# A new order of the same operations on all engines, with 26 warming matmuls, in a fused attention and mixer kernel

## The chip, the cores and the metric

The kernel runs on one core of a Trainium2 chip. The metric is device time in microseconds (us), the median of three runs. Beside the runs there is one profiled execution with a trace of every engine and DMA queue.

## What is computed

Eight batches, eight heads, a sequence of 576 and a head dimension of 64. Attention is causal by blocks of 64: a query sees the keys of its own block and of the earlier ones. A mixer follows, first along the sequence (256 hidden), then along the channels (1536 hidden), with a residual each:

```python
scores = scale * np.matmul(q, k.transpose(0, 1, 3, 2))
mask = block_i >= block_j
attn = np.exp(scores - max) / (sum + 1e-09)          # masked scores are -1e9
x = np.matmul(attn, v)                               # as (batch, 576, 512)
h = np.maximum(x.transpose(0, 2, 1) @ w_tok1, 0.0) @ w_tok2
u = x + h.transpose(0, 2, 1)
h2 = np.maximum(u @ w_ch1, 0.0) @ w_ch2
return u + h2
```

Inputs and the output are float32.

## The kernel before

The whole kernel is a list of some 1500 operations (`Plan`, `P.add`). One operation is a small piece of work on one engine: a set of score matmuls, an exponential, a load, an evacuation of a PSUM bank. Each states its dependencies, the engines that it may run on, and the banks that it takes and gives back.

Which engine runs an operation, which bank it gets and where it stands are written out in one long string, `ORDER` (L97 to L178), and `Plan.placed()` walks along it. A word of it is the operation's number, a letter for the engine (T TensorE or PE, A ScalarE or ACT, D VectorE or DVE, P GpSimd or POOL, S SyncE or SP), and one letter for each PSUM bank taken: a to d are the "mm" banks, e to h the "late" ones, s and t the two score tiles of two banks each. Each engine works through its words strictly in this order, and an instruction that waits holds up all that stands behind it on the same engine. That goes for DMA issues too: the loads of q, k, v and weights are issued by POOL or SP between that engine's other work. Nothing is decided while the kernel runs.

The stages of one batch, with their lines:

- Load: `load_qk` casts and loads q and k, L395 for the cast, L419, L426 and L437 for the DMA issues, L442 for the transposes on DVE. `load_v` is L471, the channel weights are L505 and L514.
- Attention: `score_set` (L569) makes eight or so products of 32 rows with q and k, in PSUM; an exponential on ACT (L587 and L737 in the first batch, L776 later) turns them to bf16; the end block is copied and cleared (L595, L600, `tail`); `head_out` (L617) and `ends_out` (L670) multiply by v, with a column of ones for the sum; a reciprocal and a product on DVE (L637, L643) normalize.
- Token mixing: `token_up` (L811, L815) and `token_mix` (L910). For the first batch `first_u` (L846, L859, L871) brings the result into the transposed form through PE; for later batches SP issues DMA transposes (L977, operations 606 and 607 among them).
- Channel mixing: `channel_up` (L1038), `channel_up_half` (L1111) and `channel_up_fast` (L1235) going up, with relu at L797; `first_down` (L1460) and `channel_down_fast` (L1369) going down. The fast forms save matmuls with sums of operands that DVE makes (L1351) and with folds of the products on DVE (L1393). The stores are L1421 and L1435, 128 or 256 KB or 512 KB each.

The last batches have no attention beside them, so the end of the kernel is a long row of products, folds and stores.

At the start nothing has landed yet, and PE has nothing to do. `raise_clock` gives it matmuls on a tile of zeros: `WARM` = 11 of 512 columns in one operation (43, L366), and after that single operations (44 to 80, L373) of 256 columns, "keep" matmuls, which `ORDER` strews among the first score sets. `init_tiles` (L340) clears the tile of zeros and four other tiles on DVE.

Operations that the prediction names: 17 and 14 are the first casts on ACT, 13 and 16 the loads ahead of them; 15, 18, 20, 22, 24 and 1, 2 are transposes on DVE and clears; 138, 142, 161 and 163 score sets of the first batch; 200 and 205 the two score sets behind these that take four banks each; 51 and 58 keep matmuls, 150 and 173 attention outputs, 154 and 165 likewise; 9 the clearing of the zeros; 850, 853 and 847 loads of q and k for later batches; 1460, 1462, 1492 and 1484 products of the last stage, and 1461 (which 1462 waits for), 1485 and 1475 folds there.

Of the kernel before, what the change touches and what calls it, by code (L numbers as in the profile page):

```python
# [27 lines left out]
class Plan:  # L28
# [69 lines left out]
    16S 0A 11D 10D 13S 9D 21P 1D 2D 43Ta 5D 19P 4D 3D 23P 33P 27P 14A 25P 31P 15D 29P 17A 20D 37P 44Tb 45Tb 46Tb 22D  # L98
    47Ta 36P 48Ta 49Ta 18D 50Ta 51Ta 52Ta 35P 53Ta 24D 54Ta 55Ta 56Ta 125Ts 34P 100Ttbc 179P 126A 28D 57Ta 58Ta 59Ta
    176P 60Ta 61Ta 26D 62Ta 101A 12P 106Ts 63Ta 32D 182P 64Ta 107A 65Ta 104Tt 42P 30D 66Ta 67Ta 105A 68Ta 39P 123Ts  # L100
    102D 103D 69Ta 70Ta 41P 119A 71Ta 157Tt 124A 112Td 40P 113T 116Ta 108Tb 114D 120A 38P 109T 115D 138Ts 158A 181D
    81P 72Td 73Tc 74Tc 121D 75Tc 122D 139A 82P 76Tc 7D 144Tt 110D 111D 84P 135Td 178D 127Tc 145A 161Ts 185P 136D
    117D 137D 140D 131Tb 180D 83P 128T 162A 142Tt 177D 90P 132T 129D 143A 77Td 89P 163Ts 130D 133D 86P 134D 78Td
    164A 118D 141D 159D 200Tdcba 160D 85P 203A 173Te 154Tf 165Tg 202A 91P 174D 166T 155D 156D 201A 184D 92P 205Tbhfc
    204A 183D 169Td 88P 170T 209A 167D 263Ta 168D 208A 175D 150Tc 171D 261Tg 172D 207A 187D 267Td 206A 87P 186D
    146Te 262A 147T 264A 151T 268D 237Tgbfh 152D 339P 6D 148D 269Ta 153D 241A 149D 273Td 189P 240A 270D 281Tc 239A
    274D 265Te 190P 238A 271Ta 8D 282D 275Tb 266A 191P 193Tdhfg 276A 272D 283Te 196A 277Tc 342P 194A 315Ta 278D
    306Tb 197A 188P 294Td 195A 279Tc 284A 192P 318Tf 198D 280D 291Tg 319T 348P 316T 309Tc 317A 310T 257D 93P 320A
    307T 295T 94P 308A 292T 311A 258D 225Teahf 345P 296A 300Tb 227A 95P 285Tc 228A 286T 293D 226A 303Td 287D 229A
    304T 351P 232Tahge 341D 199D 312Tc 230D 233A 305D 313T 234A 231D 288Tf 344D 314A 297Ta 340D 236A 289T 343D 235A  # L110
    210Td 513P 245Tc 290A 211D 213Th 516P 212D 242Te 246D 216Tg 354P 247D 301T 214D 215D 248Td 243D 302A 298T 244D
    355P 217D 219Tc 249D 299A 250D 222Th 220D 254Te 221D 363Tdbaf 255D 256D 251Tc 349D 364A 330Te 352P 252D 365A
    218D 253D 321Td 367A 223D 224D 366A 259D 353P 368Tcghb 420Ta 372A 370A 422Tb 347D 371A 525P 346D 322T 421D 423A
    260D 369A 356Tafgh 323T 359A 357A 350D 424Tb 360A 324D 331T 358A 425D 388Tcadg 361P 514D 430Tb 391A 434Th 332T
    389A 431D 435A 518D 426Td 392A 517D 400Thcbf 390A 515D 428Tg 404A 393P 362D 334Ta 522P 403A 429D 677P 401A 335T
    333D 402A 528P 427D 376Tb 373Tc 394D 527P 96D 395Tdfgh 379Te 526P 377D 396A 374D 336T 375D 397A 519P 378D 380D
    405Tc 398A 680P 381D 382Tb 399A 406D 385Td 407D 432Te 337D 417Tc 383D 386D 433A 530Tafgh 387D 384D 418D 436Td
    419D 531A 440Tb 97D 414Tc 534A 325Te 533A 98D 326T 532A 415D 437A 416D 542Tahgf 99D 441A 438Tc 545A 327T 439D
    544A 444D 463Tgd 543A 445D 448Thb 328D 466A 464Tc 451D 546A 329S 411Ta 408Te 465A 446D 469T 412D 690P 413D 449Tf
    523D 470A 454T 529P 450A 409D 442Ta 410D 452Tc 455A 443D 691P 467Tg 520D 453A 537Taefh 447D 692P 468A 456T 521D  # L120
    538A 473T 689P 524D 539A 471T 679D 540A 683P 596Ta 457D 541A 474D 562Tcefh 597A 678D 458T 566A 681D 594Ta 565A
    459D 564A 460D 476T 563A 595D 461T 477A 569Tchfe 682D 462A 472D 604Ta 847P 571A 478Tdb 475D 686P 572A 605D 602Tg
    535P 481A 600Th 603D 536P 570A 598Ta 567P 482Tf 601D 607S 568P 553Tc 844P 599D 483A 479Tg 550Th 554D 555D 480A
    488T 551D 484T 552D 606S 489D 486T 485A 556Tc 487D 491T 573A 574Thadg 557D 490D 492A 547Te 558D 577A 493D 497Tbf
    575A 548D 576A 549D 559Tc 578A 688D 701Tedah 498A 685D 579Tg 560D 704A 684D 499T 705A 494D 850P 702A 693P 580D
    585Ta 703A 581D 503T 500D 687D 706Tgdbh 586D 587D 561D 591Te 504D 710A 501Ta 709A 495D 708A 592D 707A 593D 582Tc
    502D 627Tbd 612The 608D 630A 588Tg 583D 496D 505T 859P 615D 858P 633T 584D 506D 507T 857P 634A 589D 590D 860P
    694Tcgab 508D 856P 618T 698A 849D 509T 697A 846D 696A 619D 695A 760Tb 609D 610D 699P 510D 738Tacgh 761A 848D
# [42 lines left out]
    1457D 1392D 1492The 1453D 1393T 1488D 1493A 1489D 1455D 1498T 1394D 1458T 1396S 1460T 1490D 1459D 1472Tca 1468D  # L171
    1465S 1461D 1494T 1464S 1473A 1469D 1476Td 1470D 1478T 1491D 1462T 1479D 1471D 1499D 1482T 1463D 1496Tg 1477D
    1466S 1483D 1502T 1467S 1497D 1484T 1503D 1500T 1507S 1485D 1495D 1480T 1487S 1501D 1474T 1506S 1481D 1504T
    1475D 1486S 1505D 1508S
"""


@with_exitstack  # L178
def kernel(
# [93 lines left out]
    BANK = ("mm", "late mm", "full", "late")  # L273
# [1310 lines left out]
```

## Time and profile before

| what | value |
|---|---|
| runs | 284.08, 284.12 and 285.28 us, median 284.12 |
| span of the profiled execution | 284.7 us (0.2% above the median; no other time is listed for it) |
| granted TensorE clock, each window | 1.00 |
| busy: PE, weight loads, DVE, ACT, POOL | 275.8, 197.6, 240.3, 180.4, 71.7 us |
| matmuls on PE | 4038, of them 46 on zeros |
| moved by DMA | 31.79 MB |

A row of the profile's timeline gives start and length in us, the engine, the line, the operation with output and inputs, the tile shape, and a count where equal instructions stand together; in brackets is the idle time of the engine just before, with what ended it. "issue" there means that the profile shows nothing that the engine waited for. A row of PE's waits names the line that waited, what for, the total in us, how often, and the longest. A window's row begins with its bounds and length, then busy time and count for PE, weight loads, DVE, ACT and POOL, the granted clock, the share of DMA, and GB/s. The queue q8 carries the instructions themselves from memory.

### The profile page before, as it was taken

How to read it: one execution, taken by the hardware profiler on the slowest of the kernel's cores; microseconds unless marked ns; L12 is line 12 of the kernel's file. 1: busy time of each engine (PE TensorE's matmuls, PEld its weight loads, DVE VectorE, ACT ScalarE, POOL GpSimd, SP SyncE). 2: the span in 40 equal slices, each digit the busy share in tenths (PEclk: the TensorE clock that was granted, in tenths of full speed). 3: DMA queues.
4: the chain of work that ended last, by engine and by line, in shares of the span. 5: the costliest groups of instructions: out<-in, count | busy, mean ns of one | idle time of the engine just before them, and what ended most of it. 6: DMA issues, size and time to landing. Idle time of an engine off the chain costs nothing.

```text
span 284.7 us, 9438 instructions
## 1 busy us (share of the span) xinstructions
PE 275.8 (97%) x4038; PEld 197.6 (69%) x4038; DVE 240.3 (84%) x519; ACT 180.4 (63%) x325; POOL 71.7 (25%) x120
## 2 busy tenths in 40 slices
PE   7998999999999899999999999999999999999994
PEld 3667656556878676987777658744488876468883
DVE  3589569799999799999998997997998987598893
ACT  3798685778888358996879785136546653764000
POOL 8975635170641062060341220000000000000000
PEclk9999999999999999999999999999999999999999
DMA  8999999969989495898199587130033403000246
GB/s 160 166 174 202 190 205 203 137 94 134 144 120 119 71 84 87 225 135 122 11 169 102 87 106 132 49 119 18 2 74 98 126 7 131 12 2 0 104 127 212
DMA packets 64776, 31.79 MB, mean 112 GB/s; under 512 B 53088, under 2 KB 55904, under 8 KB 64736
## 3 DMA queue, kind: packets, MB, share of 16 engines
q0 software_dynamic: 45040, 17.64, 53.1%
q1 hardware_dynamic: 19696, 13.57, 19.6%
q8 instruction: 31, 0.51, 0.7%
q14 instruction: 9, 0.07, 0.1%
HBM read 35.85 MB, written 9.44 MB: 159 GB/s over the span
## 4 chain that ended last, share of the span: by engine, by line
PE 92%; DVE 2%; ACT 2%; DMA 1%; issue 1%; SPq 0%; DVEq 0%
PE late L1369 14%; PE mm L1369 11%; PE late L1235 7%; PE mm L1111 7%; PE late L1111 6%; PE mm L569 6%; PE mm L1235 6%; PE mm L617 4%; PE mm L811 3%; PE mm L910 3%; PE mm L1038 3%; PE late L569 2%; PE late L617 2%; PE late L811 2%; PE mm L1460 2%; PE late L1460 2%
## 5 line engine op out<-in xcount | busy, mean ns | idle before, releaser
L776 ACT ACTIVATE e_sb<-late 128x512 bf16<-128x512 f32 x89 | 50.5, 609 | 10.4 <-PE late L569 9.1
L776 ACT ACTIVATE e_sb<-mm 128x512 bf16<-128x512 f32 x79 | 45.1, 609 | 9.9 <-PE late L569 6.6
L471 POOL DMA_DIRECT2D vals<-in_v_dram x45 | 37.2, 844 | 26.7 <-PE late L617 15.9
L442 DVE STREAM_TRANSPOSE qk_sb<-qk_sb 128x288 int32<-128x288 int32 (+2 forms) x57 | 36.2, 694 | 4.6 <-ACT qk_sb L395 3.5
L1369 PEld LDWEIGHTS <-sums 128*128 128x128 bf16 x288 | 27.6, 98 | 5.6 <-issue 1.8
L1369 PEld LDWEIGHTS <-gT 128*128 128x128 bf16 x288 | 27.8, 98 | 4.6
L569 PEld LDWEIGHTS <-qk_sb 32*64 32x64 bf16 x1280 | 19.9, 104 | 13.1 <-issue 8.8
L569 PE MATMUL mm<-qk_sb 32*64 32x64 bf16 (+7 forms) x546 | 27.8, 291 | 0.0
L569 PE MATMUL late<-qk_sb 32*64 32x512 bf16 (+7 forms) x594 | 27.1, 291 | 0.0
L617 PEld LDWEIGHTS <-e_sb 128*128 128x128 bf16 x640 | 23.8, 97 | 4.1 <-issue 0.9
L1111 PEld LDWEIGHTS <-ws_sb 128*128 128x128 bf16 x192 | 17.8, 98 | 3.4 <-issue 1.3
L797 ACT ACTIVATE gT<-mm 128x512 bf16<-128x512 f32 x25 | 14.7, 601 | 7.8 <-PE mm L1111 3.0
L617 PE MATMUL mm<-vals,e_sb 128*128 128x65 bf16 x430 | 19.0, 193 | 0.0
L643 DVE TENSOR_TENSOR x_sb<-mm,rinv 128x256 bf16<-128x256 f32 x43 | 17.9, 421 | 1.1
L1111 PEld LDWEIGHTS <-wc_sb 128*128 128x128 bf16 x144 | 15.4, 114 | 1.8 <-issue 0.2
L1235 PEld LDWEIGHTS <-ws_sb 128*128 128x128 bf16 x96 | 9.3, 98 | 10.1 <-issue 0.2
L1369 PE MATMUL late<-wd_sb,sums 128*128 128x256 bf16 x108 | 13.6, 272 | 1.2 <-issue 1.2
L1369 PE MATMUL late<-wd_sb,gT 128*128 128x256 bf16 x120 | 14.7, 273 | 0.0
L595 POOL COPY vals<-e_sb 128x256 bf16<-128x256 bf16 x10 | 4.1, 412 | 40.9 <-issue 22.9
L395 ACT COPY mm<-late 128x512 f32<-128x512 f32 x17 | 9.9, 584 | 7.1 <-PE late L1235 5.0
L797 ACT ACTIVATE gT<-late 128x512 bf16<-128x512 f32 x17 | 10.2, 602 | 6.3 <-PE late L1235 3.4
L1235 PE MATMUL late<-e_sb,ws_sb 128*128 128x512 bf16 x44 | 12.6, 379 | 0.0
(203 smaller groups left out, 656.2 us busy)
## 6 DMA issues: line engine op xcount, KB each, us to landing
out_dram<-o_sb SPq DMA_DIRECT2D x14, 512.0 KB, 3.1
vals<-in_v_dram POOLq DMA_DIRECT2D x28, 128.0 KB, 5.4
qk_sb<-in_k_dram POOLq DMA_DIRECT2D x12, 288.0 KB, 6.3
qk_sb<-in_q_dram POOLq DMA_DIRECT2D x12, 288.0 KB, 5.9
out_dram<-o_sb SPq DMA_DIRECT2D x7, 256.0 KB, 3.2
wc_sb<-in_moe_w_ch_dram POOLq DMA_DIRECT2D x8, 192.0 KB, 7.7
wc_sb<-in_moe_w_ch_dram POOLq DMA_DIRECT2D x3, 512.0 KB, 10.4
vals<-in_v_dram POOLq DMA_DIRECT2D x15, 64.0 KB, 4.9
```

The source lines that it names most:

```text
L442: nc.vector.transpose(dst[:, 0:S, :] .rearrange("p s e -> p (s e)") .bitcast(I32) .rearrange("p (a k) -> p k a", k=NB)[:, k0:k1], raw2.bit ...
L471: nc.gpsimd.dma_start(out=t[128 - p : 128, J, hs, 0:64], in_=src)
L569: nc.tensor.matmul(out=home(n)[64 * half : 64 * half + 64, c : c + w], lhsT=bar[r, 0] if j is None else kT[i][r, 64 * j : 64 * j + 64, par ...
L617: nc.tensor.matmul(out=u[:, I, 0:65], lhsT=e[:, h, c : c + 128], rhs=vt[:, J, head, 0:65], start=(J == 0), stop=(J == I),)
L643: nc.vector.tensor_tensor(out=xt[:, 0:4, 64 * head : 64 * head + 64], in0=u[:, :, 0:64], in1=ri[:, 0:4].to_broadcast([128, 4, 64]), op=MULT,)
L776: nc.scalar.activation(dst, bank_of(x), EXP, scale=scale)
L797: nc.scalar.activation(dst, src, RELU)
L811: nc.tensor.matmul(out=ps, lhsT=w1_sb[:, c, tt : tt + 255 : 2], rhs=xt[:, c, cols], start=(c == 0), stop=False)
L1111: nc.tensor.matmul(out=bank_of(bank)[:, 256 * o_ : 256 * o_ + 256], lhsT=x(o_, m), rhs=y[:, :, m, :], start=opens, stop=m == 1, skip_group ...
L1235: nc.tensor.matmul(out=bank_of(bank), lhsT=x(m), rhs=y[:, :, m, :], start=first and m == 0, stop=m == 1, skip_group_check=not first,)
L1369: nc.tensor.matmul(out=bank_of(bank)[:, 256 * i : 256 * i + 256], lhsT=x[:, kk, 128 * i : 128 * i + 128], rhs=y[:, kk], start=first and i ...
L1460: nc.tensor.matmul(out=ps, lhsT=gT[0][:, cc, 128 * si : 128 * si + 128], rhs=wc2_sb[:, cc, :], start=cc == 0, stop=cc == NDC - 1,)
```

## The change

`ORDER` is replaced as a whole. The operations are the same except for the keep matmuls, and each still stands behind all that it depends on; place, bank and in some 80 cases the engine (among DVE, ACT and POOL) are new. Three stores (1465, 1486, 1507) move from SP to ACT. The keep matmuls get two widths: three of four are 512 columns wide, every fourth 256. `ORDER` uses 26 of them (16 wide, 10 narrow) where it used 35 narrow ones. PE has 4029 matmuls instead of 4038. The first 11 warming matmuls stay.

```diff
 ORDER = """
-    16S 0A 11D 10D 13S 9D 21P 1D 2D 43Ta 5D 19P 4D 3D 23P 33P 27P 14A 25P 31P 15D 29P 17A 20D 37P 44Tb 45Tb 46Tb 22D
-    47Ta 36P 48Ta 49Ta 18D 50Ta 51Ta 52Ta 35P 53Ta 24D 54Ta 55Ta 56Ta 125Ts 34P 100Ttbc 179P 126A 28D 57Ta 58Ta 59Ta
...
+    3D 11D 23P 4D 10D 21P 7D 16S 13S 0A 17A 19P 14A 9D 43Ta 29P 35P 5D 18D 1D 59Tb 15D 60Tb 31P 65Tb 24D 2D 22D 48Tb
+    47Tb 20D 125Ts 80Tb 126A 27P 25P 100Ttbc 61Td 101A 36P 37P 56Td 106Ts 34P 44Td 72Td 49Td 63Td 107A 123Tt 33P
+    119A 124A 104Ts 62Td 54Td 46Td 52Td 179P 55Td 28D 26D 32D 30D 144Tt 57Td 120A 121D 122D 131Td 132T 105A 145A
+    102P 103P 176P 133D 127Tc 128T 41P 138Ts 129D 130D 139A 157Tt 181D 134D 116Tc 180D 135Tb 178D 136D 38P 158A 185P
+    64Ta 108Ta 39P 182P 117D 142Ts 118D 143A 112Td 113T 40P 109T 177D 161Tt 76Tc 68Tc 45Tc 42P 137D 163Ts 50Tc 81P
+    110D 84P 114D 115D 111D 187D 162A 164A 200Tcadb 202A 204A 8D 186D 205Tefgh 208A 203A 51Ta 58Ta 82P 159D 83P 140D
...
-    1465S 1461D 1494T 1464S 1473A 1469D 1476Td 1470D 1478T 1491D 1462T 1479D 1471D 1499D 1482T 1463D 1496Tg 1477D
-    1466S 1483D 1502T 1467S 1497D 1484T 1503D 1500T 1507S 1485D 1495D 1480T 1487S 1501D 1474T 1506S 1481D 1504T
-    1475D 1486S 1505D 1508S
+    1394D 1396S 1456T 1458T 1457D 1459D 1460T 1461D 1464S 1489D 1492Tgf 1490D 1462T 1493A 1498T 1491D 1465A 1496Ta
+    1463D 1466S 1467S 1499D 1476Te 1469D 1470D 1471D 1497D 1478T 1502T 1503D 1507A 1479D 1494T 1495D 1500T 1504T
+    1505D 1508S 1482T 1477D 1483D 1474T 1501D 1480T 1481D 1506S 1484T 1485D 1487S 1475D 1486A
 """
...
         for n in range(KEEP):
             bank = {"covers": False}
-
-            def emit(o, bank=bank):
+            w = 512 if n % 4 else 256
+
+            def emit(o, bank=bank, w=w):
                 nc.tensor.matmul(
-                    out=bank_of(bank)[:, 0:256], lhsT=zeros[:, 0:128], rhs=zeros[:, 0:256],
-                    start=True, stop=True,
+                    out=bank_of(bank)[:, 0:w], lhsT=zeros[:, 0:128], rhs=zeros[:, 0:w], start=True, stop=True,
                 )
...
-                "PE", 0.11, emit, pads["zeros"], 1e6, take=[(BANK, bank)], give=[bank], at=5.0 + 0.12 * n, until=20.0,
+                "PE", mm_cost(w, 1), emit, pads["zeros"], 1e6, take=[(BANK, bank)], give=[bank], at=3.0, until=20.0,
                 quick=True,
```

More of the change, by code (lines that the diff above doesn't have):

```diff
@@ L103 @@
[L103 to L127, printed above, removed]
@@ new lines @@
+    369A 356Taech 516P 349D 303Td 304T 305D 350D 420Tf 421D 358A 360A 359A 355P 257D 514D 93P 301T 302A 522P
+    388Tcdhe 392A 390A 391A 357A 361P 306Tf 307T 389A 308D 422Te 423A 400Tfhdb 401A 402A 404A 94P 291Ta 258D 259D
+    292T 293D 426Te 403A 518D 430Tf 395Thcga 399A 397A 432Tb 398A 362P 385Td 297Ta 298T 515D 299A 433A 431D 95P 517D
+    680P 424Tg 382Tc 427D 386D 425D 383D 384D 379Te 380D 387D 373Ta 288Tb 396A 289T 290A 376Tc 530Tdhgf 531A 436Tb
+    374D 375D 381D 330Te 434Ta 525P 532A 428Th 523D 677P 529P 524D 686P 393D 394P 331T 534A 527P 437D 429D 435D
```

109 lines of the change are left out of this document (62 added, 47 removed).

## The prediction

> **What bounds the kernel now.** I read the page first, then PE's waits, then the windows, then the timeline of PE around each wait.
>
> ```profile
> span 284.7 us, 9438 instructions
> PE 275.8 (97%) x4038; PEld 197.6 (69%) x4038; DVE 240.3 (84%) x519; ACT 180.4 (63%) x325; POOL 71.7 (25%) x120
> PE 92%; DVE 2%; ACT 2%; DMA 1%; issue 1%; SPq 0%; DVEq 0%
> ```
>
> The first line is the span, the second the busy time, the third the chain that ended last by engine. TensorE (PE) is busy for 97% of the span and is 92% of the chain: the other engines matter only where they make PE wait. PE's waits are few:
>
> ```profile
> PE mm L366 <- DVE wd_sb L340: 1.7, 1, 1.7
> PE late L1369 <- issue: 1.2, 1, 1.2
> PE late L815 <- issue: 0.7, 1, 0.7
> PE sc L569 <- DVE qk_sb L442: 0.5, 1, 0.5
> PE mm L811 <- DVE x_sb L643: 0.3, 1, 0.3
> ```
>
> Two of them (1.7 and 0.5) belong to the start. Behind it stand 1.2, 0.7 and 0.3, and two of these are "issue": nothing that the profile shows held PE. The windows (PE's busy time and count are the first figures after the length) say the same stage by stage:
>
> ```profile
> 0.00:20.80 20.80, 18.41 (x322) 11.04 (x322) 12.07 (x42) 14.36 (x18) 17.90 (x34) 1.00 1.25 166
> 20.80:27.70 6.90, 6.87 (x157) 5.61 (x157) 6.28 (x20) 6.19 (x14) 4.08 (x7) 1.00 1.13 201
> 27.70:31.00 3.30, 2.57 (x73) 2.22 (x74) 1.66 (x5) 2.33 (x5) 2.41 (x4) 1.00 1.17 210
> 31.00:93.20 62.20, 62.13 (x1079) 40.89 (x1078) 55.04 (x127) 48.57 (x94) 24.95 (x39) 1.00 1.25 146
> 93.20:280.60 187.40, 185.85 (x2408) 137.84 (x2407) 164.85 (x328) 108.93 (x197) 22.39 (x37) 1.00 0.49 88
> ```
>
> From 20.8 us on PE is idle for 0.03 + 0.73 + 0.07 + 1.55 us. An order can win only this, something of the start, and something of the 4.1 us from 280.6 to the end.
>
> **Where the idle time is.** PE's timeline around the three, and what the instruction queue q8 moved just before two of them (from 25.9 to 27 and from 92 to 93 us; no packet of q8 from 21 to 25.9, none from 81 to 92):
>
> ```profile
> 28.43 0.20 PE L815 MATMUL late<-x_sb,w1o_sb 128*128 128x64 bf16 x1 [0.75 <-issue]
> 94.37 0.60 PE L1369 MATMUL late<-wd_sb,sums 128*128 128x256 bf16 x4 [1.24 <-issue]
> 148.44 0.81 PE L811 MATMUL mm<-x_sb,w_sb 128*128 128x512 bf16 x3 [0.31 <-DVE x_sb L643]
> q8 instruction: 1, 0.02, 5.3%
> q8 instruction: 1, 0.02, 6.0%
> q8 instruction: 31, 0.51, 0.7%
> ```
>
> The last line is the whole run: 31 packets, 0.51 MB, so 16 KB each. PE runs 4038 matmuls and as many weight loads, 8076; over 31 that is about 256 a packet, 128 matmuls. The windows place the two stalls: up to 27.70 PE has run 322 + 157 = 479 matmuls, 958 instructions; up to 93.20 another 73 + 1079, in all 3262. 958 is 4 x 256 less 66, and 3262 is 13 x 256 less 66. Both stand at the same place of a block, nine blocks apart, and each ends about 1.4 us after a packet of q8. I read them as PE waiting for its next 256 instructions. [...]
>
> If a block is asked for when PE enters the one ahead of it (the trace does not show the request), the first was asked for at 351 matmuls, some nine past 21.25 us, and came in the window from 25.9: over 4 us late, with the loads of q and k, v and the channel weights in flight. The second was asked for near 86.5 us, 134 matmuls before 93.2, and came after 92: over 5 us late, behind these:
>
> ```profile
> 83.42 4.29 SPq L977 DMA_TRANSPOSE uT<-u_sb  x2
> 83.99 0.53 POOL L419 DMA_DIRECT2D qk_sb<-in_k_dram  x1
> 86.50:93.20 6.70, 6.63 (x134) 5.09 (x133) 6.63 (x16) 5.63 (x11) 1.23 (x2) 1.00 1.40 100
> ```
>
> So a stall needs two things: loads and DMA transposes queued when a block is asked for, and a block that PE runs through quickly (6 to 7 us or less).
>
> **The change part by part.**
>
> *Fetch stalls.* The real matmuls are the same 3992; nine keep matmuls fewer shift each boundary by 18 instructions. In the new order the transposes 607 and 606 and the loads 850, 853 and 847 fall in a block that holds 64 product matmuls and is long (by the spacing that its operations have in the old timeline some 10 us). Nothing asks for a block right behind that queue with a short block to cover it. I take -1.24 and -0.75, and -0.31 for the third, which ends in the same manner. Between them -2.3.
>
> *New stalls.* The new order has two short blocks, its fourth and fifth: 80 score matmuls, 36 of first_u and 12 of token_up in the latter. The window from 27.7 to 31 runs such work at 2.57 us for 73, so 128 take about 4.5 us. Behind loads as dense as at 21 us (over 4 us late, about 1 us of data, 1.4 us to restart) PE would wait 2 to 2.5 us. But there the order lets POOL issue eight loads just ahead of the boundary and then none for over 100 matmuls; with nothing in flight the wait is zero. Ends 0 and 2.5; I take +0.5, nearer to zero because the queue runs dry in that block.
>
> *The start.* Rows of it:
>
> ```profile
> 1.33 0.27 DVE L340 MEMSET wd_sb<- 128x256 uint32 x1
> 5.20 1.25 ACT L395 CAST qk_sb<-gT 128x576 bf16<-128x576 f32 x2 [2.95 <-DMA gT<-in_k_dram]
> 5.90 2.88 DVE L442 STREAM_TRANSPOSE qk_sb<-qk_sb 128x288 int32<-128x288 int32 x6 [3.51 <-ACT qk_sb L395]
> 6.16 1.58 PE L373 MATMUL mm<-wd_sb 128*128 128x256 bf16 x13
> 8.29 0.42 PE L569 MATMUL sc<-qk_sb 32*64 32x512 bf16 x6 [0.54 <-DVE qk_sb L442]
> 8.98 3.84 ACT L587 ACTIVATE e_sb<-sc 128x1024 bf16<-128x1024 f32 x4 [2.54 <-PE sc L569]
> 12.72 0.59 ACT L737 ACTIVATE e_sb<-mm 128x512 bf16<-128x512 f32 x1
> 13.19 1.03 ACT L587 ACTIVATE e_sb<-sc 128x1024 bf16<-128x1024 f32 x1
> 16.70 4.05 ACT L587 ACTIVATE e_sb<-sc 128x1024 bf16<-128x1024 f32 x4 [0.15 <-PE sc L569]
> 17.63 0.47 PE L617 MATMUL mm<-vals,e_sb 128*128 128x65 bf16 x10
> 18.04 0.39 PE L569 MATMUL sc<-qk_sb 32*64 32x448 bf16 x2
> 20.77 2.56 ACT L776 ACTIVATE e_sb<-mm 128x512 bf16<-128x512 f32 x5
> ```
>
> Load, cast, transpose, first score set at 8.29, exponentials from 8.98 to 20.75 us: ACT sets the pace of the start. Wide exps take 0.935 us (four from 8.98 to 12.72), half ones 0.47 (12.72 to 13.19): eleven and two are 11.2 us, and they take 11.77, so 0.55 is slack. The new order casts what lands first and needs one transpose (2.88/6 = 0.48) fewer ahead of the first score set: -0.4. But it puts 138 behind two head outputs and others, 142 behind four short operations, 161 behind three, 163 behind keep matmuls. A head output is 0.41 us (17.63 to 18.04), a keep of 512 columns about 0.2: I estimate 0.5 + 0.4 + 0.35 + 0.2 = 1.45 of waits of ACT, of which 0.55 only replaces the slack. Last wide exp: -0.4 + 1.45 - 0.55 = +0.5.
>
> Then 205 (banks e to h) follows straight on 200 (a to d), where before 173, 154 and 165 stood between them. All eight banks are full, and what comes next (51, 58, 150, 173) waits for exps at 2.56/5 = 0.51 us a bank. I take +0.6 (0 to 1.0). Together the start is **+1.1**, bounds -0.4 (the gain alone, all waits covered) and +2. The warming matmuls (26 instead of 35, 16 of them 512 wide) cost nothing of their own: they fill time in which PE would wait for ACT. At 0.11 us (13 in 1.58) for 256 columns and twice that for 512 they are 16 x 0.22 + 10 x 0.11 = 4.6 us, the price without that cover; before they were 35 x 0.11 = 3.9. Those in front of score sets are counted above. The zeros that they read are cleared sixth on DVE and not third, about 0.6 us later than 1.33 + 0.27.
>
> *Engines exchanged.* About 80 small operations change between DVE, ACT and POOL. DVE (84%) and ACT (63%) have room over the span; I cost them at nothing, and without that cover at up to +1 between 21 and 50 us, where ACT gets its exps earlier and is nearly full.
>
> *Inside the tail.* Rows:
>
> ```profile
> 271.63 0.69 DVE L1393 TENSOR_TENSOR o_sb<-mm,o_sb 128x512 f32<-128x512 f32 x1
> 279.06 0.82 PE L1369 MATMUL mm<-wc_sb,vals 128*128 128x256 bf16 x6
> 279.72 0.82 PE L1369 MATMUL late<-wd_sb,vals 128*128 128x256 bf16 x6
> 280.57 0.42 DVE L1393 TENSOR_TENSOR o_sb<-late,e_sb 128x256 f32<-128x256 f32 x1 [0.23 <-PE late L1369]
> out_dram<-o_sb SPq DMA_DIRECT2D x7, 256.0 KB, 3.2
> out_dram<-o_sb SPq DMA_DIRECT2D x2, 128.0 KB, 2.6
> ```
>
> In the new order 1462 needs the fold 1461 of product 1460, with only the half product 1492 (279.06 to 279.72, 0.66) between: 0.23 + 0.69 - 0.66 = **+0.27** of wait. At the end the last product 1484 is followed by two folds in a row, 1485 and 1475 (the second some 0.35 later), and the last store is 256 KB (3.2 us to landing) where it was 128 KB (2.6): +0.35 + 0.6 at most, +0.35 at least as SP and ACT now issue the last two side by side. I take **+0.6**.
>
> *Sum.* -2.3 + 0.5 + 1.1 + 0.27 + 0.6 = +0.17 on the span of 284.7: 284.87. The profiled span is 0.58 above the median of the runs, 284.12; on that scale the forecast is **284.3**. A measurement of this kernel tells about 0.5% (1.4 us) from no change, so "same" is 282.7 to 285.5.
>
> **The rivals.**
>
> A, *the start gains too.* The score sets run ahead of the exps far enough that the head outputs between them hide, and the bank waits are covered: start -0.4, no new fetch stall. -2.3 - 0.4 + 0.27 + 0.6 = -1.8: 282.3. For it: the 3.9 us of keep matmuls in before show that PE has time to spare up to 20.8. Against: ACT's chain has two score buffers only (s and t). 0.2.
>
> B, *slower: the fetch stall moves.* One mechanism: the block asked for at the entry of the short fifth block (some 4.5 us, near 27 us) sits behind the eight loads of v, q and channel weights issued just ahead. It decides as soon as that packet comes over 2 us late; at the 4 us and more of before it costs 2.5 instead of 0.5: +2.2, 286.3. For it: DMA is full in this stretch (1.13 of 16 engines' share). Against: the pause in POOL's issues. 0.18.
>
> C, *the start costs 2 us* and ACT, full from 21 on, loses another 0.4: +1.5, 285.6. 0.09.
>
> D, *the stalls don't go.* [...] The place in the block and the packets speak against it: 0.03. [...]
>
> [...]
>
> **How the numbers follow.** Forecast 0.5, A 0.2, B 0.18, C 0.09, D 0.03. Slower by over 0.5% is B, C and D: 0.3; faster is A: 0.2; within 0.5% is 0.5. Sure bounds of the costs: start -0.4 to +2, new stalls 0 to 2.5, tail 0.35 to 0.95, so 282.0 to 287.5; the range 282.2 to 286.9 leaves out the outer edges of A and B. Of it, the likeliest case by itself holds 282.7 to 285.5.
>
> **What would show it.** Right: no "issue" wait of PE over 0.5 us behind 20 us; the first score set at about 7.9, the last wide exp over at about 21.2; 1462's wait of 0.2 to 0.3 near the end; the last store landing about 0.6 later behind PE's last matmul. Wrong: an "issue" wait near 27 to 32 us with a q8 packet just ahead of it (B), exps without gaps from the first score set on (A), long waits of PE for ACT between 20 and 30 us (C), the 1.24 still there (D). The forecast fails most easily by the start, whose +1.1 is the least sure term.

## The result, and the profile after

| | before | changed |
|---|---|---|
| median of the runs, us | 284.18 (4 runs, 284.08 to 285.28) | 288.11 (4 runs, 286.95 to 289.54) |
| ratio to before | | 1.0131 (95% interval 1.0095 to 1.0167) |
| span of the profiled execution | 284.7 | 286.7 |
| time of that execution | some 286.5 (below) | 288.55 |

The change makes the kernel 1.3% slower; the forecast was 284.3 with a range up to 286.9. The spans of the two profiles differ by 2.0 us, the medians by 3.9. Most of that lies in the profile of before. Later comparisons list time and span of each run of before: 284.29 with 282.5, 284.97 with 283.2, 284.12 with 282.4. The time is 1.7 to 1.85 us above the span in all of them (1.85 in the changed kernel's profiled execution). By that a span of 284.7 is a time of about 286.5, an estimate, since no time is listed for this execution. Of the 23 runs of before in the first of these comparisons only two were longer: what I took for a usual execution was a long one.

The page of the changed kernel:

```profile
span 286.7 us, 9402 instructions
PE 277.7 (97%) x4029; PEld 197.5 (69%) x4029; DVE 242.1 (84%) x527; ACT 175.0 (61%) x318; POOL 71.1 (25%) x119
PE 92%; ACT 2%; DVE 2%; issue 2%; DVEq 0%
```

TensorE (PE) is the bound as before, at the same share. PE's waits of the changed kernel (line that waited, what for, total in us, times, longest):

```profile
PE mm L365 <- DVE wd_sb L339: 2.2, 1, 2.2
PE mm L568 <- issue: 1.9, 1, 1.9
PE late L669 <- issue: 0.3, 1, 0.3
PE late L568 <- ACT e_sb L586: 0.2, 1, 0.2
```

The three waits of 1.24, 0.75 and 0.31 are gone. A new "issue" wait of 1.9 us stands in a score set (L568), and one of 0.3 at 155 us. Its place, and the instruction queue just before it (the first row is a window from the start to it; the next two are the timeline around it; then q8 from 31.3 to 32.4; from 26.2 to 31.3 there is no packet of q8):

```profile
0.00:31.70 31.70, 29.17 (x607) 18.08 (x608) 20.71 (x65) 24.48 (x38) 25.30 (x48) 1.00 1.31 160
31.56 0.19 PE L568 MATMUL mm<-bar 32*64 32x64 bf16 x2
33.61 0.22 PE L568 MATMUL mm<-qk_sb 32*64 32x64 bf16 x2 [1.86 <-issue]
q8 instruction: 1, 0.02, 5.5%
```

607 matmuls are 1214 instructions, 5 x 256 less 66: the same place of a block as the two stalls of before. The packet came after 31.3 us, four us after PE entered the block ahead (at 27.4 us, 128 matmuls earlier), and PE went on 1.3 us after it had landed (at 32.3). This is rival B, where the prediction put it. The traces show no request; I count it from PE's entry into the block ahead. In the first profiles of both kernels PE enters 31 blocks (at the 95th matmul and every 128 from there) and q8 has 31 packets; taken in order, the first ten start 0.1 to 4.3 us after the entry, the others between 2.0 us before it and 5.2 after. POOL's timeline shows which loads were issued around 27.4 us, the request by this count:

```profile
24.48 0.57 POOL L418 DMA_DIRECT2D qk_sb<-in_q_dram  x1
25.62 1.78 POOL L470 DMA_DIRECT2D vals<-in_v_dram  x2
27.39 1.64 POOL L504 DMA_DIRECT2D wc_sb<-in_moe_w_ch_dram  x3
29.95 0.40 POOL L594 COPY vals<-e_sb 128x256 bf16<-128x256 bf16 x1 [0.92 <-ACT e_sb L775]
```

Load 342 (q) and two loads of v stand ahead of the request, three weights right behind it. POOL's pause, on which the prediction counted, begins at 29.0 us, after the request. How short the blocks are here is seen in how many matmuls stand in the stretch from 24 to 41 us; first the changed kernel, then before:

```profile
24.00:41.00 17.00, 15.14 (x419) 12.40 (x415) 13.32 (x43) 12.89 (x26) 10.14 (x20) 1.00 1.37 183
```

```profile
24.00:41.00 17.00, 16.25 (x272) 10.71 (x270) 11.50 (x27) 12.86 (x27) 9.41 (x14) 1.00 1.42 198
```

The new order brings score sets and head outputs, many small matmuls, into this stretch: 419 instead of 272. A block of 128 matmuls lasts about 5 us instead of 8 on average, with the DMA share nearly as large (1.37 and 1.42). From 41 to 130 us PE has no idle time at all:

```profile
41.00:130.00 89.00, 89.00 (x1451) 63.61 (x1440) 80.69 (x178) 65.13 (x126) 32.18 (x49) 1.00 0.93 134
```

The start of the changed kernel, DVE, PE and ACT:

```profile
7.30 0.72 DVE L441 STREAM_TRANSPOSE qk_sb<-qk_sb 128x288 int32<-128x288 int32 x1 [0.70 <-DMA qk_sb<-in_q_dram]
8.41 0.65 PE L568 MATMUL sc<-qk_sb 32*64 32x512 bf16 x8
9.10 2.86 ACT L586 ACTIVATE e_sb<-sc 128x1024 bf16<-128x1024 f32 x3 [3.88 <-PE sc L568]
18.94 2.15 ACT L586 ACTIVATE e_sb<-sc 128x1024 bf16<-128x1024 f32 x2 [0.17 <-PE sc L568]
21.14 0.66 PE L568 MATMUL late<-qk_sb 32*64 32x512 bf16 x16 [0.22 <-ACT e_sb L586]
21.73 0.82 PE L373 MATMUL mm<-wd_sb 128*128 128x512 bf16 x3
```

In this execution the first score set comes at 8.41 and not earlier than before (8.29): the transpose at 7.30 waited for a load. In a second profile of the same kernel, further down, it comes at 7.06. The last wide exponential ends at 21.09 (before 20.75). Then 205 waits 0.22 us, and three keep matmuls follow it.

The end of the changed kernel:

```profile
272.29 0.82 PE L1368 MATMUL late<-wc_sb,vals 128*128 128x256 bf16 x6
273.23 1.47 PE L1368 MATMUL late<-wd_sb,gT 128*128 128x256 bf16 x12
282.60 0.42 DVE L1392 TENSOR_TENSOR o_sb<-mm,e_sb 128x256 f32<-128x256 f32 x1 [0.23 <-PE mm L1368]
282.94 0.41 DVE L1392 TENSOR_TENSOR o_sb<-late,e_sb 128x256 f32<-128x256 f32 x1
```

Product 1462 begins 0.94 us behind 1492 (0.66 would be dense). The last fold ends at 283.35, and the span ends 3.35 us later; before it was 280.99 and 3.7 us. From PE's last matmul to the end it is 4.1 us in the changed kernel and 4.2 before (280.54 to 284.7).

### The profile page after: what moved, and what is told of

The parts are those of the page before. It is cut to its first block, busy times and chain, and to the rows that moved or that the text cites. A ratio compares the mean times of both kernels' runs of the same rounds, so it can differ in the third digit from the quotient of the medians.

```text
span 286.7 us, 9402 instructions
## 1 busy us (share of the span) xinstructions
PE 277.7 (97%) x4029; PEld 197.5 (69%) x4029; DVE 242.1 (84%) x527; ACT 175.0 (61%) x318; POOL 71.1 (25%) x119
## 4 chain that ended last, share of the span: by engine, by line
PE 92%; ACT 2%; DVE 2%; issue 2%; DVEq 0%
PE mm L1368 14%; PE late L1368 11%; PE late L1234 6%; PE mm L1234 6%; PE late L1110 6%; PE mm L1110 5%; PE late L568 4%; PE mm L616 4%; PE mm L568 4%; PE late L909 3%; PE mm L1037 3%; PE late L810 3%; PE late L616 3%; PE sc L568 2%; PE mm L810 2%
## 5 line engine op out<-in xcount | busy, mean ns | idle before, releaser
L775 ACT ACTIVATE e_sb<-mm 128x512 bf16<-128x512 f32 x86 | 48.5, 608 | 10.1 <-PE mm L568 6.0
L775 ACT ACTIVATE e_sb<-late 128x512 bf16<-128x512 f32 x82 | 47.2, 611 | 7.5 <-PE mm L568 4.6
L1368 PEld LDWEIGHTS <-gT 128*128 128x128 bf16 x288 | 27.7, 98 | 5.0 <-issue 0.3
L568 PE MATMUL mm<-qk_sb 32*64 32x64 bf16 (+7 forms) x622 | 28.0, 284 | 2.0 <-issue 1.9
L568 PEld LDWEIGHTS <-qk_sb 32*64 32x64 bf16 x1280 | 20.0, 104 | 13.8 <-issue 10.3
L568 PE MATMUL late<-qk_sb 32*64 32x512 bf16 (+7 forms) x518 | 27.1, 300 | 0.2 <-ACT e_sb L586 0.2
L796 ACT ACTIVATE gT<-mm 128x512 bf16<-128x512 f32 x23 | 13.6, 605 | 7.6 <-PE mm L1037 2.9
L418 POOL DMA_DIRECT2D qk_sb<-in_k_dram x12 | 6.6, 546 | 46.0 <-DVE th_sb L1082 20.9
L616 PE MATMUL mm<-vals,e_sb 128*128 128x65 bf16 x390 | 17.4, 193 | 0.0
L642 DVE TENSOR_TENSOR x_sb<-mm,rinv 128x256 bf16<-128x256 f32 x39 | 15.9, 417 | 0.8
L1368 PE MATMUL mm<-wd_sb,sums 128*128 128x256 bf16 x120 | 14.7, 273 | 0.0
L394 ACT COPY late<-mm 128x512 f32<-128x512 f32 (+1 forms) x14 | 7.9, 569 | 10.2 <-PE mm L1368 4.3
L394 ACT COPY late<-late 128x512 f32<-128x512 f32 (+1 forms) x11 | 6.1, 564 | 13.1 <-PE late L1368 8.1
L924 DVE TENSOR_TENSOR u_sb<-late,x_sb 128x512 bf16<-128x512 f32 x17 | 11.5, 685 | 2.8 <-PE late L909 2.6
```

The costliest lines, as they stand in the source:

```text
L394: nc.scalar.copy(dst, src)
L568: nc.tensor.matmul(out=home(n)[64 * half : 64 * half + 64, c : c + w], lhsT=bar[r, 0] if j is None else kT[i][r, 64 * j : 64 * j + 64, par ...
L616: nc.tensor.matmul(out=u[:, I, 0:65], lhsT=e[:, h, c : c + 128], rhs=vt[:, J, head, 0:65], start=(J == 0), stop=(J == I),)
L642: nc.vector.tensor_tensor(out=xt[:, 0:4, 64 * head : 64 * head + 64], in0=u[:, :, 0:64], in1=ri[:, 0:4].to_broadcast([128, 4, 64]), op=MULT,)
L775: nc.scalar.activation(dst, bank_of(x), EXP, scale=scale)
L796: nc.scalar.activation(dst, src, RELU)
```

## The experiments

Each group of runs was compared with before on one chip, and there were four chips, on which before has medians from 284.8 to 285.1. The changed kernel was run again on one of them and has 288.38 there. In brackets stand the ratio to before on the same chip and its 95% interval; runs on different chips are compared by these ratios (0.001 is 0.3 us). Where a run has six samples they spread by 1.4 to 4.3 us; differences under half a microsecond are not read.

**Stores on one queue or two.** The changed kernel with its ACT stores on SP, and before with the same three on ACT:

```diff
-1465A ... 1507A ... 1486A
+1465S ... 1507S ... 1486S
```

> The changed kernel with its three ACT stores (1465, 1486, 1507) back on SP, nothing else moved. The changed kernel's profiled execution took 288.55 us with a span of 286.7, 1.85 outside the span; the kernel before took 284.1 to 285.3 with a span of 284.7. Theory 1: a second store queue costs about 1.4 us outside the span; then this kernel comes to about 286.7 us, and its time stands within 0.6 us of its span. Theory 2: the stores' engine is of no account and the whole loss is inside the span; then 288.1 within 0.4.

Measured: 288.66 (1.0121, 1.0098 to 1.0144), span 286.9 with a time of 289.03. The second store queue costs nothing outside the span: with SP alone the time is 2.1 us above it. Theory 1 falls, and with it the thought that the 1.85 us outside the span belong to the change: before has 1.8 as well. The profile of this run is worth more than its time:

```profile
PE mm L1037 <- DMA wc_sb<-in_moe_w_ch_dram: 1.0, 1, 1.0
PE late L669 <- issue: 0.3, 1, 0.3
PE late L669 <- DMA vals<-in_v_dram: 0.3, 1, 0.3
PE mm L568 <- issue: 0.2, 1, 0.2
```

Here the stall in L568 is 0.2 us instead of 1.9, with nothing changed ahead of it: the packet came 2.3 us after its request instead of 4.0. But the first channel products (L1037) wait 1.0 us for a channel weight instead, and nothing is gained.

> The kernel before with the same three stores on ACT instead of SP. Theory 1 (second store queue costs outside the span): about 285.6 us, 1.4 above before, with the span unchanged at 284.1 to 284.7. Theory 2: 284.2 within 0.3.

Measured: 284.1 against 284.97, ratio 0.9962 (0.9939 to 0.9986). The number is theory 2's, but before has 284.97 on this chip, so two store queues gain 0.9 us in the kernel before (0.4 to 1.7 by the interval), against both theories. In the changed kernel the same exchange shows no gain (1.0121 without it, 1.0131 and 1.0126 with it). This version of before beats both kernels. The last fold of its profile, and of the run with the changed order and all stores on SP:

```profile
279.81 0.42 DVE L1393 TENSOR_TENSOR o_sb<-late,e_sb 128x256 f32<-128x256 f32 x1 [0.23 <-PE late L1369]
282.68 0.42 DVE L1392 TENSOR_TENSOR o_sb<-late,e_sb 128x256 f32<-128x256 f32 x1
```

From there to the end of the span it is 3.1 us (span 283.3) and 3.8 us (286.9). With the 3.7 of before and the 3.35 of the changed kernel, the second issuing engine saves 0.5 to 0.6 us at the end in both orders.

**The queue ahead of the fetch.** Nine memsets on POOL ahead of load 342, and six ahead of load 90 in before:

```diff
...
+            for _ in range(BRAKE.get(op.n, 0)):      # BRAKE = {342: 9}, in before {90: 6}
+                nc.gpsimd.memset(brake, 0.0)
             op.emit(op)
```

> The changed kernel with nine small memsets on POOL ahead of load 342, some 2 us in which POOL issues no load, so that fewer loads are queued when PE asks for its instructions at about 27.4 us. Theory 1: the 1.86 us idle stretch of PE at 31.75 is a fetch that waits behind the loads in flight; then it falls below 0.5 us, the packet of q8 comes at about 29 instead of 31.4, and the time falls by 1.2 to 1.8 to about 286.5. Theory 2: the stretch is a wait of score set 232 for something the profile doesn't show, or a fetch that takes its time whatever is in flight: the stretch stays over 1.3, and the loads that come later make the time 288.1 or more.

Measured: 290.78 (1.0187, 1.0158 to 1.0216). The stall in the score set is gone, as theory 1 says, but the time is no shorter: it is 2.1 us above the run with the SP stores on the same chip (288.66). PE's waits:

```profile
PE late L670 <- DMA vals<-in_v_dram: 2.1, 1, 2.1
PE late L670 <- issue: 1.4, 1, 1.4
```

The v loads behind the pause are now late by 2.1 us, and a later fetch costs 1.4 (at 158 us; the changed kernel has 0.3 at the same matmul). The packet of q8 started 0.7 us after PE entered the block ahead, instead of 4.0. So the length of the stall hangs on the loads issued ahead of it; but these loads are what PE needs next.

> The kernel before with six small memsets on POOL ahead of load 90, about 1.4 us without a load issued, so that the fetch of about 21.4 us finds a shorter queue. Theory 1 (fetch behind loads): the 0.75 us idle stretch at 27.7 is gone, time 284.2 - 0.75 = 283.4, unless later loads then come late. Theory 2: it stays, 284.2 within 0.3 or later.

Measured: 284.89 against 284.97, 0.9998 (0.9976 to 1.0021): no gain, as theory 2 has it. The pause stood ahead of eight weights, which POOL then issued from 21.0 to 25.2 us, around the request. The packet came 3.7 us after it, where the first profile has 4.3, and the stall at 27.7 us is still there, shorter:

```profile
PE late L816 <- issue: 0.4, 1, 0.4
PE late L618 <- DVE x_sb L699: 0.4, 1, 0.4
PE mm L812 <- DVE x_sb L644: 0.3, 1, 0.3
```

The second row stands at the 351st matmul, where a block begins too (479 less 128), so it may be a fetch as well. This profile has no stall at 93 us at all, though nothing was changed there; the one with ACT stores has 0.8 there and 0.5 at 27.7. The sum of PE's three waits in the order of before is 2.3 us in the first profile, 1.6 with ACT stores, and 1.1 in these rows.

**Weights first.**

```diff
-190P 342P 12P ... 191P ... 188P ... 90P ... 198P ... 91P 343D ... 344D ... 341D
+190P 12P ... 191P ... 188P ... 90P 91P 342P ... 198P ... 341D 343D 344D
```

> The changed kernel with load 342 (q of a later batch) issued behind channel weights 90 and 91 instead of ahead of the last v loads, 91 issued ahead of the copy 198, and the transposes 343 and 344 of that q moved behind 341. Theory A: from 25 to 41 us the changed kernel is bound by loads; the first channel products (L1037) need weight 91, which lands at 37 us whether or not PE stalls for its fetch before; then 91 lands some 1.2 us earlier, the wait for the channel weights goes, and the time falls by 0.5 to 1.2 where the fetch stall is short, less where it is long: 287.4 within 0.5, on the scale on which the changed kernel has 288.1 to 288.7. Theory B: the fetch alone costs; loads later on don't matter, and the time is that of the changed kernel within 0.3.

Measured: 289.95 (1.0162, 1.013 to 1.0194), by the ratios about 1 us slower than the changed kernel, with overlapping intervals. Both numbers fail. The fetch stall stayed at 1.6; weights now stood ahead of the packet where 342 had been. Two smaller ones (0.4 at 27.5, 1.1 at 156) came to it.

**The keep matmuls at 21.7 us.**

```diff
-51Ta 58Ta ... 53Ta
```

> The changed kernel without the keep matmuls 51, 58 and 53 (0.65 us of TensorE between 21.7 and 22.4 us). Theory A (loads bind at 37 us, and the banks before): PE gets no further, the time is that of the changed kernel within 0.3. Theory C: the start's lag on PE is carried to the end, so that 0.5 to 0.65 us come back: about 287.8.

Measured: 288.54 (1.0127, 1.0096 to 1.0157). 0.65 us less on PE bring nothing, as theory A says: in place of the three keeps PE now waits for an exponential. Further on PE waits 0.5 us after 606 matmuls, 1.3 us behind a packet of q8 (the profile puts that down to a v load), and DVE holds PE at 39 us. A row of PE's waits and one of DVE's timeline:

```profile
PE late L669 <- ACT e_sb L775: 0.7, 1, 0.7
38.98 1.26 DVE L441 STREAM_TRANSPOSE qk_sb<-qk_sb 128x288 int32<-128x288 int32 x2 [1.22 <-DMA qk_sb<-in_k_dram]
```

A transpose waits 1.22 us for the k load (339), and the reciprocals behind it on DVE wait with it. So three things that are loaded in this stretch can hold PE here: instructions, a channel weight, a k load.

**The phase of the blocks.**

```diff
-            for _ in range(WARM):
+            for _ in range(5):
                 nc.tensor.matmul(out=bank_of(bank), lhsT=zeros[:, 0:128], rhs=zeros, start=True, stop=True)
+            for _ in range(24):
+                nc.tensor.matmul(
+                    out=bank_of(bank)[:, 0:128], lhsT=zeros[:, 0:128], rhs=zeros[:, 0:128], start=True, stop=True,
+                )
```

> The changed kernel with six of its first eleven warming matmuls cut into 24 of 128 columns: as long, but 18 matmuls more, which moves each block of 256 instructions 18 matmuls back in the order. If the stall at 31.75 is an instruction fetch, a stall of PE near 31 us comes again after 607 matmuls (1214 instructions, 5 x 256 less 66), which is now 18 matmuls earlier in the work, 0.5 to 2 us long or hidden. If it is a wait of score set 232, it stays at the same matmul of that set, then the 625th. The time: the changed kernel's within 0.7 by theory A, since the loads bind behind it in either case.

Measured: 290.68 (1.0196, 1.0164 to 1.0227). The stalls of its profile, with the windows up to each:

```profile
32.00 0.39 PE L572 MATMUL late<-qk_sb 32*64 32x448 bf16 x2 [0.32 <-issue]
37.92 0.28 PE L620 MATMUL late<-vals,e_sb 128*128 128x65 bf16 x4 [1.93 <-issue]
```

```profile
0.00:31.60 31.60, 27.90 (x607) 18.82 (x608) 20.12 (x64) 24.24 (x38) 25.05 (x48) 1.00 1.30 156
0.00:35.95 35.95, 31.94 (x735) 22.56 (x736) 24.23 (x79) 28.15 (x45) 27.61 (x52) 1.00 1.29 163
```

They stand at 607 and at 735 matmuls, 128 apart, though the same counts are now 18 matmuls earlier in the work: 448 columns of the score set where it was its last 64, and a head output. The place goes by the count of instructions and not by the operation. This settles that the stalls are fetches. The time was outside theory A's 0.7: by the ratios it is about 2 us above the changed kernel, and no run shows why.

**Stores on ACT and two k loads later, in before.**

```diff
-847P ... 844P ... 850P
+850P 847P 844P
...
-1465S ... 1507S ... 1486S
+1465A ... 1507A ... 1486A
```

> The kernel before with stores 1465, 1486 and 1507 on ACT (which alone gave -0.9) and loads 847 and 844 issued behind 850, at about 91 us, so that the fetch asked for at 86.5 us has one load and the two DMA transposes ahead of it instead of three loads. If the stall at 93 us is that fetch, it is gone in every run: 0.3 to 0.9 less than with the stores alone, some 283.5 where the kernel before has 285.0. If not: as with the stores alone, 284.1.

Measured: 284.21 against 285.09, 0.9976 (0.9959 to 0.9992). The wait at 93 us is gone in the profile, but the time is no better than with the stores alone (0.9962): the expected 0.3 to 0.9 failed. What that stall costs in a usual execution of before isn't shown; of the profiles of that order that leave this place alone, three have it (1.24 and twice 0.77 us) and two don't.

**Two loads less.**

```diff
-            op.emit(op)
+            if op.n not in (339, 342):
+                op.emit(op)
```

> The changed kernel without the transfers of loads 342 and 339 (q and k of one later half batch, 288 KB each; what they should bring is left out, the transposes behind them run on what the tile holds). Theory A: between 25 and 41 us TensorE is held by what stands in the load queue, now its next block of instructions, now a channel weight; two loads take about 2.2 us of that queue (1.2 us of it ahead of the fetch of 27.4 us). Then the fetch comes 1.0 to 1.2 us earlier, the stall at 31.75 falls from 1.9 below 0.9, no wait for weights takes its place, and the time is 1.0 to 1.8 us below that of the changed kernel on the same chip. Theory B: the order of PE, ACT and DVE holds this stretch by itself; the time stays within 0.4 of the changed kernel's.

Measured: 288.62 (1.0131, 1.011 to 1.0152). Nothing came back, and theory A's number failed. The fetch stall is 1.4 us. POOL's timeline shows why:

```profile
25.46 1.77 POOL L470 DMA_DIRECT2D vals<-in_v_dram  x2
27.21 1.64 POOL L504 DMA_DIRECT2D wc_sb<-in_moe_w_ch_dram  x3
```

PE came to its block at 28.0 us, and POOL had gone on to the next loads: three weights stood ahead or beside where 342 had been. Leaving a load out did not clear the way here, since POOL issued the next one at once.

> The kernel before without the transfers of the same two loads (same part left out). Theory A: before runs only some 275 matmuls between 24 and 41 us, where the changed kernel runs 419, so its blocks of instructions are long and the queue matters little: 0 to 0.4 us faster than before. If the two loads cost both kernels alike (DMA traffic as such), it is 1 us or more faster.

Measured: 285.29 against 284.84, 1.0012 (0.999 to 1.0033). In before the two loads make no difference that can be told, as theory A has it, though its sign is not shown. The fetch stall at 28 us was 1.2 in this profile.

> The changed kernel without the transfers of loads 342 and 339 and without the keep matmuls 51, 58 and 53. Without the keeps alone nothing came back. Theory A: with the queue shorter PE can use an earlier start, 0.3 to 0.6 us less than with the two loads left out alone. If the same: the keeps fill a wait for banks that is there without them.

Measured: 287.06 (1.0089, 1.0065 to 1.0113), 1.3 below the changed kernel and 1.6 below the changed kernel without the two loads (288.62), all on one chip: more than was expected. In its profile, which is of the longest of its six executions (288.58), the packet came 1.8 us after its request, the stall was 0.6, and two more of 0.55 and 0.8 stand at later blocks. Why this run gains so much isn't shown.

> The changed kernel itself, for its time on the chip of these comparisons and a second profile of it: 288.1 to 288.9. In the profile a fetch stall of 0 to 2 us at the 607th matmul, and behind it a wait for a channel weight that is the longer the shorter the stall is; both together 1.2 to 2.2 us.

Measured: 288.38 (1.0126, 1.0098 to 1.0153). Its first score set came 1.35 us earlier than in the first profile, and the stall ended at nearly the same time (PE's timeline):

```profile
7.06 0.42 PE L568 MATMUL sc<-qk_sb 32*64 32x512 bf16 x4
33.44 0.22 PE L568 MATMUL mm<-qk_sb 32*64 32x64 bf16 x2 [2.40 <-issue]
```

The first profile has 8.41 and 33.61. Of the lead of 1.35 some 0.7 was left where the stall begins (31.04 against 31.75), and a stall of 2.40 instead of 1.86 took most of that. Between these two profiles the end was set by when the packet came, not by when PE arrived. The expected wait for a weight behind it didn't show, and the sum was 2.4 and not at most 2.2.

**Weights first with a pause.**

```diff
...
+            for _ in range(BRAKE.get(op.n, 0)):      # seven, ahead of 92
+                nc.gpsimd.memset(brake, 0.0)
```

> The changed kernel with load 342 behind channel weights 90 and 91 (as in the run with the weights first) and seven small memsets on POOL ahead of weight 92, some 1.6 us in which no load is issued, so that the five v loads come as early as before and the fetch of 27.4 us finds only them ahead. Theory A (the stall is the queue that stands ahead of the fetch): the packet starts by 30.2 us instead of 31.2 to 31.5, the stall at the 607th matmul falls below 0.9, and the time is 0.3 to 1.2 below that of the run with the weights first (289.95), about 289. If the stall stays at 1.5 or more with an earlier packet, PE waits for something else.

Measured: 290.21 (1.018, 1.013 to 1.0229): not faster. The packet came at 29.3 and the fetch's stall is gone, as expected; PE's waits show what took its place and a later fetch, at 158 us, and DVE's timeline what is behind the first:

```profile
PE late L569 <- DVE rinv L637: 2.6, 1, 2.6
PE late L670 <- issue: 1.4, 1, 1.4
```

```profile
39.70 2.34 DVE L442 STREAM_TRANSPOSE qk_sb<-qk_sb 128x288 int32<-128x288 int32 x4 [2.15 <-DMA qk_sb<-in_k_dram]
```

The four transposes stand in a row because the order with the weights first moved 343 and 344 behind 341; so a part of the 2.6 may belong to that order and not to the loads.

**Density under loads.** The same 144 narrow matmuls early or late in before:

```diff
...
+            if op.n in EXTRA:
+                for _ in range(12):
+                    nc.tensor.matmul(
+                        out=bank_of(op.take[0][1])[:, 0:64], lhsT=ident, rhs=ident[:, 0:64], start=True, stop=True,
+                    )
             op.emit(op)
```

> The kernel before with 144 narrow matmuls more (64 columns, on a finished tile, into a bank that is overwritten at once), twelve ahead of each of the twelve channel_up pairs of the first batch, between 30 and 41 us. It makes that stretch as dense in instructions as the changed kernel has it. They take 0.03 to 0.05 us each by themselves, 4.5 to 7 us. Theory D (density under loads: a block of 256 instructions that is run through in 4 to 5 us doesn't cover a fetch that waits for loads): stalls of 0.5 to 2 us appear there at 128 k - 33 matmuls, and the time is 1 to 3 us above that of the same 144 matmuls put at 216 to 245 us. If density doesn't matter, the two are within 0.6 of each other.

> The kernel before with the same 144 narrow matmuls ahead of twelve products between 216 and 245 us, where no loads are in flight: the price of the matmuls themselves, 4.5 to 7 us above before, and no stall by a fetch in that stretch.

Measured: early 291.53 (1.0218, 1.0168 to 1.0267), late 289.65 (1.0156, 1.012 to 1.0192). (In the late one the matmuls overwrite some banks that already hold a part of a sum.) The matmuls alone cost 4.6 us; under loads it is 1.9 more, as theory D has it, though the intervals just overlap. The stretch of the early and of the late one, and the window of the early one up to its stall:

```profile
24.00:41.00 17.00, 15.95 (x322) 11.66 (x320) 8.79 (x19) 11.05 (x24) 9.42 (x14) 1.00 1.43 199
```

```profile
24.00:41.00 17.00, 17.00 (x280) 11.16 (x278) 12.23 (x28) 13.67 (x29) 9.43 (x15) 1.00 1.43 199
```

```profile
0.00:32.79 32.79, 29.48 (x607) 20.50 (x607) 21.04 (x68) 24.47 (x38) 26.21 (x47) 1.00 1.24 180
```

The loads are the same (1.43 and 199 GB/s in both). With 322 matmuls PE idles 1.05 us, nearly all of it (0.98) at the 607th matmul; with 280 it does not idle at all.

**All three relieved.**

```diff
...
+            if op.n == 92:
+                for _ in range(7):
+                    nc.gpsimd.memset(brake, 0.0)
-            op.emit(op)
+            if op.n not in (339, 342):
+                op.emit(op)
```

> The changed kernel without the transfers of loads 342 and 339 (what they bring is left out) and with a pause of some 1.6 us in POOL's load issues ahead of channel weight 92. Then each of the three things that were seen to hold TensorE between 30 and 41 us finds less ahead of it: the fetch of the 607th matmul, channel weight 91, and the k load that the transposes on DVE wait for. Theory A (the three stand in one load queue, and each shows when the one before it is taken away): no stall over 0.6 us between 30 and 41 us, time 286.2 to 287.2, 1.2 to 2.2 below the changed kernel's 288.4. Theory B (the order itself): within 0.5 of 288.4.

> The same without the keep matmuls 51, 58 and 53. Theory A: with the queue out of the way TensorE is the bound from 21.7 us on and the 0.65 us of keeps come back in part: 0.3 to 0.6 below the run with the two loads and the pause alone. Theory B: no difference.

Measured: 287.47 (1.0089, 1.0068 to 1.0111) and, without the keeps, 287.19 (1.0083, 1.0051 to 1.0115). PE's waits of the first:

```profile
PE late L670 <- issue: 0.9, 1, 0.9
PE sc L569 <- DVE qk_sb L442: 0.5, 1, 0.5
PE mm L1038 <- DMA wc_sb<-in_moe_w_ch_dram: 0.4, 1, 0.4
```

From 30 to 41 us PE idles 0.4 us (the weight) where the changed kernel idles 1.9 and 2.4 in its two profiles; the 0.9 is the fetch near 154 us. So theory A is right on the idle time. The time falls by about 1 us by the ratios (1.0126 to 1.0089, with overlapping intervals), 0.9 from 288.38, between the two theories' numbers. The keeps bring 0.3, too little to tell.

## Why the prediction was wrong

**The base.** The step that failed first is "the profiled span is 0.58 above the median of the runs": it set a span beside times. The time is 1.8 above the span, so that execution was some 2.4 us above the median. Of the miss of 3.8 us (288.1 against 284.3) these 2.4 are the larger part, and they are why the measured time lies even above the sum of the sure bounds, 287.5. The stalls that I took as a gain of 2.3 were those of a long execution; five other profiles of that order, each with a small edit, have 1.1 to 2.0 us of waits behind the start in sum. Against the median there was less to win.

**Fetch stalls.** The mechanism was right and is now shown: the place by count (607 and 735 matmuls, 479 and 1630 before: multiples of 128 less 33, once less 34; the prediction's windows count one matmul at their edges twice and make it 1631), the packet, and the phase. All three waits went, as the prediction said, but the third is no fetch: 0.31 or 0.32 us by DVE stand there, two or three matmuls ahead of a block, in every profile of that order, so "ends in the same manner" misread it. Rival D falls: the two "issue" waits of before, 1.24 and 0.75 us, are not in the changed kernel's profile. The packets behind the stalls came 4.0 us (changed), 4.3 and 5.2 us (before) after PE entered the block ahead, and the stalls last up to 2.40 us (second profile of the changed kernel).

**New stalls, +0.5.** This term failed worst: 1.86 in the profile, 2.40 in the second, 0.2 in one whose packet happened to come earlier. The failed step is "I take +0.5, nearer to zero because the queue runs dry in that block". POOL's pause comes after PE's request; what counts is what was issued before it, 342 and two v loads from 24.5 to 27.4 us. The runs with a pause there bear it out: their packets came 0.7 to 1.9 us after the request, those of the changed kernel and of the runs that leave these loads alone 2.1 to 4.5. Rival B with 286.3 was right in place, price (2.5 at most) and sign, and had a chance of 0.18. On the scale of the profiles the miss of the sum is 286.7 - 284.87 = 1.8, of which this term is 1.4, and 0.3 more with the fetch at 155 us.

**But the fetch is not the whole of it.** B took the fetch as a thing by itself. But v, the channel weights and a k load, which PE needs within 2 to 8 us of it, are loaded in the same stretch. In the profiles where the fetch's wait was gone or short another stood in its place (2.1 for v, 1.0 for a weight, 2.6 by way of DVE), and the time was no shorter. With two loads left out it fell by about 1 us in three runs, with a pause (0.9), without the three keeps (1.3) and with both (1.2); with the two loads alone it did not. The cause one level up is, as far as shown, the order: it sets 419 matmuls into a stretch in which 272 stood, while the loads come no faster (183 GB/s against 198), and 144 matmuls more in before cost 1.9 us more under loads than without.

**The start, +1.1.** The exponentials end 0.34 us later, not 0.5, but both parts of that are off, so the nearness is luck. The gain of 0.4 failed in the first profile because a transpose waited for load 19, which the new order issues third on POOL; in the second the first score set came 1.2 earlier than before. And from the first score set to the end of the last wide exponential it takes 12.7 us in both, 12.5 before: 0.2 more, where I had 0.9. What the start costs at the end isn't settled, though: a start 1.35 us earlier and three keeps less brought nothing to the end. I added terms along PE where a later wait takes up the first.

**1462.** +0.27 predicted, 273.23 - 272.29 - 0.66 = 0.28 measured.

**The end, +0.6.** Nothing instead of +0.6: from PE's last matmul to the end it takes 4.1 us, before 4.2. The second fold came 0.34 us later as predicted. But from the last fold to the end it takes 3.35 instead of 3.7 us. The larger last store does cost something, 0.1 us where SP issues all (3.8 against 3.7) and 0.25 where ACT helps (3.35 against 3.1); the second issuing engine saves 0.5 to 0.6, which I had not counted.

**What stays open.** On the scale of the two profiles the known parts are -2.3 for the waits that went, +1.86 and +0.27 for the new fetch stalls, +0.28 for 1462 and nothing for the end: +0.1 of the 2.0 us between the spans. The other 1.9 is the start (forecast +1.1) and whatever else there is. By the two pages it isn't idle time: PE idles 8.9 us before and 9.0 after, and its busy time is 275.8 and 277.7 us, for the same real matmuls and wider keeps. Against a usual execution of before, whose waits are shorter, the new stalls weigh more. No run took the rest apart.

## What to carry to other kernels

Set a profiled span beside spans and a time beside times before anything is added up; a profile of one execution may be a long one, and its stalls are then larger than those that a change can win. When many small instructions are moved into a stretch with a full load queue (here 419 matmuls instead of 272 in 17 us, at a DMA share of 1.37), count blocks of instructions (here 256, by stalls 128 matmuls apart at 607 and 735) against the loads that are issued before PE enters the block ahead of each. Where instructions, weights and operands are loaded at the same time, taking one wait away may only show the next: relieve all of them in one run before pricing any.

## What was not expected of the hardware

A block of instructions came late where loads were issued just before PE entered the block ahead: 4.0 us after that entry behind 342 and two v loads, 0.7 with a pause in place of a part of them. The profile lists loads (q0) and instructions (q8) as separate queues; that one waits for the other is inferred from these times. PE went on 1.3 us after the packet had landed (32.3 and 33.6 us in the changed kernel's first profile). The same kernel's runs spread from 286.95 to 289.54, and the stall at the 607th matmul from 0.2 to 2.4 us between profiles with the same loads ahead; no run shows why.
